# Memory recalls in products of 64 features, two halves of TensorE's rows at a time, and three sums of x moved to GpSimd

## The chip, the cores and the metric

One core of one Trainium2 chip runs the whole program. The metric is the device time of one execution in microseconds (us), the median of several runs. TensorE multiplies, VectorE, ScalarE and GpSimd work on tiles, SyncE issues the transfers.

## What is computed

`x` has 2048 rows (tokens) and 576 columns (features). The output mixes two branches by a gate per token:

```python
g = sigmoid((x * gate_w).sum(-1, keepdims=True))
out = g * A(x) + (1 - g) * B(x)          # B: (gelu(x @ w_gate) * (x @ w_up)) @ w_down, 4608 wide
```

`A` is attention with 32 heads of 18 features, in 4 segments of 512 tokens, with a memory that is carried from segment to segment:

```python
phi = lambda t: where(t > 0, t + 1.0, exp(t))
M, z = zeros, zeros                       # per head: 18 x 18 and 18
for s in range(4):
    a_dot = softmax(qs @ ks.T * scale + mask) @ vs          # within the segment
    a_mem = (phi(qs) @ M) / (phi(qs) @ z + 1e-6)            # the recall
    outs.append(sigmoid(beta) * a_mem + (1 - sigmoid(beta)) * a_dot)
    M = M + phi(ks).T @ vs
    z = z + phi(ks).sum(0)
A = concat(outs) @ wo
```

The recall `phi(qs) @ M` and its denominator `phi(qs) @ z` are what the change touches.

## The kernel before

The program begins with the projections. For each segment `s` from 1 on there are four "rows" steps (`q` = 0 to 3, 128 tokens each), in which the values are projected (`vrows`, `put_rows`), the key features of the segment before are turned (`key_rows`) and added to the memory (`memorize`), and the recall of the segment before is made (`recall(p, q)` with `p = s - 1`); then nine products `project(s, j)` give the columns of q and k, which `put_columns` splits into f16 words and turns into `phi`. The recalls of segment 3 come last: two together in step `j = 6`, one in `j = 7`, one after `j = 8`. Segment 0 has no memory to recall, so there are 3 x 4 = 12 recalls. After the projections the feed-forward branch and the attention run together in `step(v)` to the end; the first `step` begins with `first_product`, whose result in the PSUM bank V VectorE copies out (L1339) before more is added to V.

All four compute engines follow the order in which the program text issues (`manual_schedule`). `later` is a list of closures: work on a product's result is put there and issued at the next `finish_later()`.

For the recall, the 576 features lie in five tiles of 128 partitions (`SPANS`). `phi[s, j]` holds tile `j` as fp32, 128 features x 512 tokens; the fifth has the last 64 features of q in its upper half and the first 64 of k, for which `bd` is zero, in its lower. `bd[:, j]` holds, as fp32, the memory of the heads that tile `j` touches, block by block: for each of up to 8 heads (`HEADS`) 18 columns of `M` and one of `z` (`MC` = 19), zero outside the head's own features. One recall is five products with 128 tokens of `phi` as weights and 152 columns of `bd` (76 for the last tile) streaming. Tiles 0 to 2 add up in one PSUM bank, 3 and 4 in another; head 21 lies in both, and `put_recall` adds its two parts, then forms denominators, reciprocals and scaled results, which go to DRAM (`oms`).

`form_sums(p, i, half, by)` makes sums of x for later products: a subtraction of 1024 columns on the engine `by` (L482), a cast by ScalarE (L484), the low words by VectorE (L486). `half` says which of these: 0 the subtraction and the cast, 1 the low words, 2 the cast alone, -1 the subtraction alone. `beside_rows` and `behind_rows` call it in the rows steps. PSUM has eight banks: `st` and `dn` two each, G, U, V and `pv` one each.

The functions that the diff touches, with the lines of the profile:

Of the kernel before, what the change touches and what calls it, by code (L numbers as in the profile page):

```python
# [8 lines left out]
F32 = mybir.dt.float32  # L9
# [4 lines left out]
OP = mybir.AluOpType  # L14
# [4 lines left out]
P = 128  # L19
D = 576  # L20
F = 4608
H = 32
DH = 18
L = 512
NH = D // 2
KT = 5
# [11 lines left out]
GN = 20  # L38
MC = DH + 1
SPANS = [(128 * j, min(128, D - 128 * j)) for j in range(KT)]  # L40
HS = 21
HEADS = [(a // DH, (a + w - 1) // DH + 1) for a, w in SPANS]


# [1 line left out]
def kernel(ctx: ExitStack, tc: tile.TileContext, xs, wqk, wv, wo, wgu, wd, beta, out):  # L46
    nc = tc.nc
    pe, act, dve, pool, sp = nc.tensor, nc.scalar, nc.vector, nc.gpsimd, nc.sync
# [425 lines left out]
    def form_sums(p, i, half, by=dve):  # L474

        r, sc = sums_x[p], xsc[:, 2 * p : 2 * p + 1]
        t = kept["xt"][p] if half >= 0 else None
        k, o, a, b = ((0, (1, 1), (1, 2), (1, 1)), (2, (1, 2), (2, 2), (1, 2)), (1, (2, 2), (2, 2), (1, 1)))[i]
        if t is not None:
            hi, lo = (flat(t[:, 4 * k + j : 4 * k + j + 2]) for j in (0, 2))  # L480
        if half <= 0:
            by.tensor_tensor(r[o], r[a], r[b], OP.subtract)  # L482
        if half == 0 or half == 2:
            act.activation(hi, r[o], AF.Copy, scale=sc)  # L484
        if half == 1:
            dve.scalar_tensor_tensor(lo, r[o], sc, hi, OP.mult, OP.subtract)  # L486
# [12 lines left out]
    qks, vps, oms, oas = [], [], [], []  # L499
# [8 lines left out]
    gh = cst.tile([P, 2, H], F32, name="gh")  # L508
# [17 lines left out]
    with tc.tile_pool(name="prj", bufs=2, side="right", reuse_waits="tile") as pp:  # L526
# [10 lines left out]
        W, phi, vst, kr, mem = {}, {}, {}, {}, {}  # L537
# [139 lines left out]
        def recall(s, q, banks=(("st", 2), ("st", 2))):  # L677

            na, nb = (bank(*i) for i in banks)

            for j, (h0, h1) in enumerate(HEADS):
                o, lo = (na, 0) if j < 3 else (nb, HS)
                pe.matmul(o[:, (h0 - lo) * MC : (h1 - lo) * MC], phi[s, j][:, q * P : (q + 1) * P],
                          bd[:, j, : (h1 - h0) * MC], start=j in (0, 3), stop=j in (2, 4), skip_group_check=True)
            later.append(lambda: put_recall(s, q, na, nb))

        def put_recall(s, q, na, nb):
            hf, c = divmod(s, 2)
            t = 4 * c + q
            dn = pp.tile([P, H], F32, name="den", bufs=2)  # L690
            rd = pp.tile([P, H], F32, name="rden", bufs=2)
            mo = pp.tile([P, D], F32, name="mo", bufs=2)
            both = na[:, HS * MC : (HS + 1) * MC]
            dve.tensor_copy(mo[:, :MC], nb[:, :MC])
            dve.tensor_tensor(both, both, mo[:, :MC], OP.add)
            parts = []
            for o, h0, h1 in ((na, 0, HS + 1), (nb, HS + 1, H)):
                o = o[:, (MC if h0 else 0) :][:, : (h1 - h0) * MC]
                parts.append((o.rearrange("p (h d) -> p h d", d=MC), slice(h0, h1), h1 - h0))
            for o, hs, n in parts:  # L700
                dve.tensor_scalar(dn[:, hs].unsqueeze(2), o[:, :, DH:], 1e-6, None, OP.add)
            dve.reciprocal(rd, dn)
            dve.tensor_tensor(rd, rd, gh[:, 0], OP.mult)
            for o, hs, n in parts:
                dve.tensor_tensor(mo[:, hs.start * DH : hs.stop * DH].rearrange("p (h d) -> p h d", d=DH), o[:, :, :DH],
                                  rd[:, hs].unsqueeze(2).to_broadcast([P, n, DH]), OP.mult)
            sp.dma_start(oms[hf][t * P : (t + 1) * P, :], mo)

        def key_rows(s, q):
            ka, kb = bank("G") if s else bank("st", 2), bank("V")  # L710
# [66 lines left out]
        with tc.manual_schedule(engines=ORDERED):  # L777
# [91 lines left out]
            def beside_rows(s, q):  # L869
                if 0 < s < 3 and q == 0:  # L870
                    add_squares(s, range(1, KT))
                if s == 1 and q == 1:
                    add_squares(0, range(1, KT))
                if s == 1 and q == 0:
                    load_sums(0)
                if s == 1 and q == 2:
                    rescale(0)
                    rescale_words(0)
                if s == 2:
                    if q > 1:  # L880
                        form_sums(0, q - 2, 1)
                    if q:
                        form_sums(0, q - 1, 0)
                if s == 3 and q == 0:
                    rescale(2)
                    for i in range(2):
                        squares(0, 1, i, lambda o, r: square_sum(o, r, True))
            def behind_rows(s, q):
                if s == 3:
                    if q == 1:  # L890
                        scales(0)
                        scales_out(0)
                        scale_g(0)
                        scale_g(1)
                    if q < 3:
                        form_sums(1, q, -1, pool if q == 0 else dve)
                    if q == 3:
                        rescale_words(2)
                        high_g(0, 0)
                        low_g(0, 0)  # L900
# [91 lines left out]
            for s in range(4):  # L992
                p = s - 1
                if s:
                    for q in range(4):
                        pv = vrows(s, q, 0)
                        if q == 0:
                            key_scale(p)
                        if done:
                            put_columns(*done)  # L1000
                            done = None
                        finish_later()
                        put_rows(s, q, 0, *pv)
                        if s == 3 and q == 0:
                            norm_x(3, bank("V"))
                        if q:
                            key_rows(p, q - 1)
                        beside_rows(s, q)
                        finish_later()
                        if held:  # L1010
                            held.pop()()
                        behind_rows(s, q)
                        pv = vrows(s, q, 1)
                        put_rows(s, q, 1, *pv)
                        if p >= 1:
                            recall(p, q)
                        if q:
                            memorize(p, q - 1)
                    finish_later()
                    key_rows(p, 3)  # L1020
                for j in range(9):
                    if j == 1 and s:
                        make_gate(s)
                    if s and j == 0:
                        memory_scale(p)
                    if s or j > 1:
                        pr = project(s, j)
                    elif j == 0:
                        prs = project_first()
                        pr = prs[0]  # L1030
                    else:
                        pr = prs[1]
                    if s and j == 0:
                        finish_later()
                        memorize(p, 3)
                    if s == 0 and j in (2, 3, 5, 6):
                        make_qk(j + 2 + (j == 3))
                    if done and (s, j) != (0, 1):
                        for d in done if isinstance(done, list) else [done]:
                            put_columns(*d)  # L1040
                    done = [done, pr] if (s, j) == (0, 1) else pr
                    if s and j == 1:
                        keep_memory(p)
                    if s == 3 and j == 1:

                        first.close()
                        mp2 = stay.enter_context(tc.tile_pool(name="ffn2", bufs=2, reuse_waits="tile"))
                        xt.append(mp2.tile([P, 12, L], F16, name="xt1", bufs=1))
                        home.update(r=mp2)
                    beside_products(s, j)  # L1050
                    finish_later()
                    if (s, j) == (1, 3):
                        make_gate(0)
                    if s == 0 and j >= 6:
                        q = j - 5
                        pv = vrows(0, q, 1)
                        put_rows(0, q, 1, *pv)
                    if s == 3 and j == 6:
                        recall(3, 0, (("dn", 2), ("dn", 2)))
                        recall(3, 1, (("V",), ("pv",)))  # L1060
                    if s == 3 and j == 7:
                        recall(3, 2, (("dn", 2), ("dn", 2)))
# [766 lines left out]
```

## Time and profile before

| | |
|---|---|
| runs | 1555.67 us median of 3 (1555.64 to 1556.55) |
| the profiled execution | span 1553.8 us from its first to its last instruction; the profile gives no other time of it |
| TensorE (PE) | busy 1548.4 us, 12195 matmul entries |
| weight loads (PEld) | busy 955.7 us, beside the matmuls |
| VectorE (DVE) | busy 1229.3 us |
| ScalarE (ACT) | busy 1183.7 us |
| GpSimd (POOL) | busy 1305.8 us |

Times in the profile are us from the start of the span. A matmul's entry lasts until its modelled end, so entries of successive matmuls overlap; the distance from one start to the next is what a matmul costs. In a group, `out<-in` are the program's tiles, `128*128` the array's rows and columns in use, then the streaming operand. Brackets in a timeline give idle time of the engine before a row and what ended it.

### The profile page before, as it was taken

How to read it: one execution, taken by the hardware profiler on the slowest of the kernel's cores; microseconds unless marked ns; L12 is line 12 of the kernel's file. 1: busy time of each engine (PE TensorE's matmuls, PEld its weight loads, DVE VectorE, ACT ScalarE, POOL GpSimd, SP SyncE). 2: the span in 40 equal slices, each digit the busy share in tenths (PEclk: the TensorE clock that was granted, in tenths of full speed). 3: DMA queues.
4: the chain of work that ended last, by engine and by line, in shares of the span. 5: the costliest groups of instructions: out<-in, count | busy, mean ns of one | idle time of the engine just before them, and what ended most of it. 6: DMA issues, size and time to landing. Idle time of an engine off the chain costs nothing.

```text
span 1553.8 us, 33925 instructions
## 1 busy us (share of the span) xinstructions
PE 1548.4 (100%) x12195; PEld 955.7 (62%) x12196; DVE 1229.3 (79%) x3198; ACT 1183.7 (76%) x2037; POOL 1305.8 (84%) x1313
## 2 busy tenths in 40 slices
PE   9999999999999999999999999999999999999999
PEld 5665655666666566666666665666666666666577
DVE  6788976778878887878788887878787878887665
ACT  7567544888888888888888888888888888876421
POOL 3544778899898999989899989898999989899597
PEclk9999999999999999999999999999999999999999
DMA  7533341667768687778777878878687878774654
GB/s 254 195 127 125 132 150 34 122 126 140 133 131 141 130 144 130 144 126 137 132 136 126 140 139 136 135 140 151 127 138 133 144 128 141 130 136 99 120 118 138
DMA packets 472601, 210.14 MB, mean 135 GB/s; under 512 B 427632, under 2 KB 437360, under 8 KB 471920
## 3 DMA queue, kind: packets, MB, share of 16 engines
q1 hardware_dynamic: 472432, 207.97, 67.6%
q8 instruction: 96, 1.57, 0.4%
q14 instruction: 73, 0.60, 0.1%
HBM read 92.03 MB, written 27.26 MB: 77 GB/s over the span
## 4 chain that ended last, share of the span: by engine, by line
PE 94%; POOL 3%; ACT 2%; DVE 1%; issue 1%; POOLq 0%
PE dn L1228 27%; PE U L1268 22%; PE V L1268 12%; PE pv L1183 4%; PE G L385 3%; PE st L447 3%; PE dn L454 2%; PE U L1275 2%; PE dn L385 1%; PE U L447 1%; PE V L1280 1%; PE G L1280 1%; PE st L1137 1%; PE G L447 1%; PE st L1669 1%; PE V L1275 1%
## 5 line engine op out<-in xcount | busy, mean ns | idle before, releaser
L1228 PE MATMUL dn<-paird,hh 128*128 128x288 f16 x3396 | 476.5, 286 | 0.2
L1164 POOL TENSOR_TENSOR pf<-pf,ph 128x512 f16<-128x512 f32 (+1 forms) x256 | 359.2, 1403 | 94.6 <-ACT ph L1163 83.6
L1228 PEld LDWEIGHTS <-hh 128*128 128x128 f16 x3456 | 332.2, 98 | 139.1 <-issue 18.1
L1268 PEld LDWEIGHTS <-pairg 128*128 128x128 f16 x2616 | 244.0, 98 | 254.8 <-issue 18.3
L1236 DVE SCALAR_TENSOR_TENSOR acc<-dn,ev,acc 128x288 f32<-128x288 f32 x534 | 274.4, 515 | 51.4 <-PE dn L1228 42.9
L1153 ACT ACTIVATE pf<-pf,mb,esc 128x512 f32<-128x512 f32 (+3 forms) x512 | 293.0, 642 | 5.2
L1268 PE MATMUL U<-xt,pairg 128*128 128x512 f16 x864 | 209.9, 379 | 0.2 <-DVE gl L1459 0.2
L1268 PE MATMUL U<-x,pairg 128*128 128x512 f16 x840 | 204.1, 379 | 0.0
L426 POOL TENSOR_TENSOR pairg<-raw,pairg 128x640 f16<-128x640 f32 (+2 forms) x144 | 176.2, 1239 | 3.0 <-ACT pairg L418 1.5
L1163 ACT ACTIVATE ph<-pf 128x512 f16<-128x512 f32 (+1 forms) x256 | 172.4, 720 | 0.0
L1255 POOL TENSOR_TENSOR hh<-gl,hh 128x512 f16<-128x512 f32 x144 | 164.4, 1163 | 7.5 <-ACT hh L1254 7.5
L1140 DVE CUSTOM_DVE_ANT_0 pf<-st,mask 128x512 f32<-128x512 f32 (+1 forms) x256 | 157.2, 614 | 0.0
L418 ACT ACTIVATE pairg<-raw 128x640 f16<-128x640 f32 (+2 forms) x144 | 89.3, 647 | 56.6 <-POOL raw L410 36.2
L1258 ACT ACTIVATE gl<-gl,sc 128x512 f32<-128x512 f32 x144 | 97.2, 716 | 40.7 <-DVE gl L1505 30.1
L303 POOL TENSOR_SCALAR raw<-raw,sc 128x640 f32<-128x640 f32 x72 | 118.7, 1663 | 0.0
L1459 DVE COPY gl<-U 128x512 f32<-128x512 f32 x72 | 49.8, 692 | 85.4 <-PE U L1268 74.9
L1150 ACT ACTIVATE mb<-mx,esc 128x4 f32<-128x4 f32 x128 | 37.5, 293 | 103.4 <-DVE mx L1140 103.4
L1140 DVE CUSTOM_DVE_ANT_0 pf<-dn,mask 128x256 f32<-128x256 f32 (+1 forms) x192 | 67.2, 375 | 55.3 <-PE dn L1137 55.3
L1268 PE MATMUL V<-xt,pairg 128*128 128x512 f16 x432 | 105.7, 381 | 0.0
L1268 PE MATMUL V<-x,pairg 128*128 128x512 f16 x432 | 104.8, 378 | 0.0
L1254 ACT ACTIVATE hh<-gl 128x512 f16<-128x512 f32 x144 | 82.6, 616 | 16.0 <-DVE gl L1250 15.8
L1183 PEld LDWEIGHTS <-pt 128*128 128x128 f16 x2560 | 83.4, 96 | 12.3
(354 smaller groups left out, 2971.1 us busy)
## 6 DMA issues: line engine op xcount, KB each, us to landing
raw<-in_wgu_dram SPq DMA_DIRECT2D x36, 640.0 KB
rawd<-in_wd_dram SPq DMA_DIRECT2D x36, 288.0 KB
qk<-stage SPq DMA_DIRECT2D x36, 256.0 KB
qt<-qk SPq DMA_DIRECT2D x128, 72.0 KB
kt<-qk SPq DMA_DIRECT2D x128, 72.0 KB
vp<-vstage SPq DMA_DIRECT2D x16, 296.0 KB
vt<-vp SPq DMA_DIRECT2D x16, 296.0 KB
qt<-qk SPq DMA_DIRECT2D x128, 36.0 KB
```

The costliest lines, as they stand in the source:

```text
L303: pool.tensor_scalar(r, r, scl[f // 2][0][:, 0:1], None, OP.mult)
L426: pool.tensor_tensor(spot(f, *p, 1), raw_g[f][:, p[0] : p[1]], spot(f, *p, 0), OP.subtract)
L1140: dve.tensor_tensor_reduce(prob[a][:, COL[qi] : COL[qi] + (qi + 1) * P], out[qi], mask[:, L - (qi + 1) * P :], 1.0, -3e38, OP.add, OP.max, ...
L1153: act.activation(r, r, AF.Exp, bias=b[:, qi : qi + 1], scale=esc[:, 0, c : c + 1])
L1163: act.activation(h[:, cols], p[:, cols], AF.Copy)
L1164: pool.tensor_tensor(p.bitcast(F16)[:, cols], p[:, cols], h[:, cols], OP.subtract)
L1183: pe.matmul(ov, pr[:, 10 * i + COL[qi] // P + kb], v[:, 4 * e + kb, c0 : c0 + VC], start=kb == 0 and i == 0, stop=kb == qi and i == 1)
L1228: pe.matmul(o[:, :NH], hh[:, a, q * P : (q + 1) * P], w[:, b, n * NH : (n + 1) * NH], start=i == 0, stop=i == 5)
L1236: dve.scalar_tensor_tensor(av, o[:, :NH], ev, av, OP.mult, OP.add)
L1255: pool.tensor_tensor(hh[:, 1], t, hh[:, 0], OP.subtract)
L1258: act.activation(t, o, AF.Gelu_apprx_tanh, scale=scl[f // 2][0][:, 2 + c : 3 + c])
L1268: pe.matmul(o, w[:, i, (a + k) * P : (a + k + 1) * P], x[:, b + k], start=start and k == 0 and i == 0 and b == h, stop=k == 1 and i == 1, ...
```

## The change

Each product of 128 features becomes two of 64: features 0 to 63 of a tile (upper half of the array's rows) add up in bank `na`, 4 heads or 76 columns each, and features 64 to 127 in bank `nb`, 5 heads or 95 columns each; the last tile has an upper half alone. So a recall has nine products of 64 rows in place of five of 128. Every tile now has its own place in both banks, and the heads that two halves share (first and last of the five in `nb`) are added in `put_recall`: a copy of 152 columns (by ScalarE for segments 1 and 2, by VectorE for segment 3) and two adds of 76. Denominators and results are taken through views of 35 places, since the banks repeat heads in groups of 7.

Three subtractions of `form_sums` go from VectorE to GpSimd: those of sums 1 and 2 of the first pair of segments (rows steps 2 and 3 of segment 2) and of sum 1 of the second pair (rows step 1 of segment 3, now ahead of the scales). In segment 2 the cast is issued behind the second `put_rows` instead of with the subtraction.

```diff
-            for j, (h0, h1) in enumerate(HEADS):
-                o, lo = (na, 0) if j < 3 else (nb, HS)
-                pe.matmul(o[:, (h0 - lo) * MC : (h1 - lo) * MC], phi[s, j][:, q * P : (q + 1) * P],
-                          bd[:, j, : (h1 - h0) * MC], start=j in (0, 3), stop=j in (2, 4), skip_group_check=True)
+            tok = slice(q * P, (q + 1) * P)
+            for j in range(KT):
+                for h, o, c, n in ((slice(0, 64), na, 0, 4 * MC), (slice(64, P), nb, 3 * MC, 5 * MC))[: 2 if j < 4 else 1]:
+                    pe.matmul(o[:, j * n : (j + 1) * n], phi[s, j][h, tok], bd[h, j, c : c + n],
+                              start=j == 0, stop=j == (4 if c == 0 else 3), skip_group_check=True)
...
-            both = na[:, HS * MC : (HS + 1) * MC]
-            dve.tensor_copy(mo[:, :MC], nb[:, :MC])
-            dve.tensor_tensor(both, both, mo[:, :MC], OP.add)
...
+            ga = na[:, : 20 * MC].rearrange("p (g e d) -> p g e d", g=5, e=4)
+            gb = nb[:, : 20 * MC].rearrange("p (g e d) -> p g e d", g=4, e=5)
+            cut = mo[:, : 8 * MC].rearrange("p (g e d) -> p g e d", g=4, e=2)
+            (act.copy if s < 3 else dve.tensor_copy)(cut, gb[:, :, 0::4])
+            for e in range(2):
+                o = ga[:, e : e + 4, 3 * (1 - e)]
+                dve.tensor_tensor(o, o, cut[:, :, e], OP.add)
+            by = lambda t: t.rearrange("p (g e) -> p g e", e=7)
+            parts = (ga, slice(0, 5), slice(0, 4)), (gb[:, :, 1:4], slice(0, 4), slice(4, 7))
...
                     if q:
-                        form_sums(0, q - 1, 0)
+                        form_sums(0, q - 1, -1, pool if q > 1 else dve)
...
                 if s == 3:
+                    if q < 2:
+                        form_sums(1, q, -1, pool)
                     if q == 1:
                         scales(0)
                         scales_out(0)
...
-                    if q < 3:
-                        form_sums(1, q, -1, pool if q == 0 else dve)
+                    if q == 2:
+                        form_sums(1, q, -1)
...
                         put_rows(s, q, 1, *pv)
+                        if s == 2 and q:
+                            form_sums(0, q - 1, 2)
                         if p >= 1:
                             recall(p, q)
```

## Rows read from the trace of the kernel before

**Rows 1.** The page's chain that ended last, shares of the span by engine.

```profile
PE 94%; POOL 3%; ACT 2%; DVE 1%; issue 1%; POOLq 0%
```

**Rows 2.** Busy times by stretch: us, busy per engine (x instructions), clock, DMA.

```profile
178.00:212.40 34.40, 34.38 (x188) 18.81 (x186) 32.99 (x65) 22.15 (x37) 21.98 (x19) 1.00 0.41 135
```

**Rows 3.** TensorE's timeline, recalls at 102 and 172 us: start us, us, what.

```profile
102.21 1.37 PE L683 MATMUL st<-bd,phi 128*128 128x152 f32 x10
103.42 0.29 PE L454 MATMUL U<-wv,x 128*128 128x288 f16 x1
...
172.08 1.37 PE L683 MATMUL st<-bd,phi 128*128 128x152 f32 x10
```

**Rows 4.** Weight loads at the end of the recall at 197 us.

```profile
197.97 0.19 PEld L683 LDWEIGHTS dn<-bd,phi 128*128 128x128 f32 x1
198.08 0.30 PEld L683 LDWEIGHTS V<-bd,phi 128*128 128x128 f32 x2
```

**Rows 5.** TensorE's timeline, fp32 products with 128 and with 64 rows.

```profile
12.92 0.65 PE L674 MATMUL pv<-acc,raw 128*128 128x288 f32 x2
...
14.08 0.40 PE L674 MATMUL V<-acc,raw 64*128 64x288 f32 x1
14.09 0.40 PE L674 MATMUL pv<-acc,raw 64*128 64x288 f32 x1
14.33 0.40 PE L674 MATMUL V<-acc,raw 64*128 64x288 f32 x1
...
14.66 0.76 PE L674 MATMUL G<-acc,raw 128*128 128x290 f32 x2
```

**Rows 6.** Weight loads of the products with 64 rows.

```profile
13.49 0.30 PEld L674 LDWEIGHTS dn<-acc,raw 64*128 64x128 f32 x4 [0.39 <-issue]
13.84 0.19 PEld L674 LDWEIGHTS V<-acc,raw 64*128 64x128 f32 x1
```

**Rows 7.** TensorE's timeline, end of the projections.

```profile
196.93 1.37 PE L683 MATMUL dn<-bd,phi 128*128 128x152 f32 x10
...
199.40 3.19 PE L447 MATMUL U<-x,wp 128*128 128x512 f16 x14
202.60 1.45 PE L683 MATMUL dn<-bd,phi 128*128 128x152 f32 x10
...
210.71 1.46 PE L1268 MATMUL V<-x,pairg 128*128 128x512 f16 x6
```

**Rows 8.** VectorE's timeline, last rows step.

```profile
171.11 0.68 DVE L724 SCALAR_TENSOR_TENSOR krow<-G,kmc,krow 128x448 f16<-128x448 f32 x1 [0.19 <-ACT krow L720]
...
173.79 0.17 DVE L694 COPY mo<-st 128x19 f32<-128x19 f32 x1
```

**Rows 9.** VectorE's timeline, end of the projections.

```profile
200.57 0.16 DVE L694 COPY mo<-dn 128x19 f32<-128x19 f32 x1
200.76 0.18 DVE L695 TENSOR_TENSOR dn<-dn,mo 128x19 f32<-128x19 f32 x1
200.98 0.26 DVE L701 TENSOR_SCALAR den<-dn 128x22 f32<-128x22 f32 x2
...
203.05 0.18 DVE L701 TENSOR_SCALAR den<-V 128x22 f32<-128x22 f32 x1
...
209.94 0.68 DVE L1339 COPY gl<-V 128x512 f32<-128x512 f32 x1
...
213.93 0.69 DVE L1459 COPY gl<-U 128x512 f32<-128x512 f32 x1 [1.97 <-PE dn L99]
```

**Rows 10.** ScalarE's groups, 98 to 125 us: busy us, mean ns, idle.

```profile
L720 ACT ACTIVATE krow<-V,kmc 128x128 f16<-128x128 f32 x4 | 1.4, 359 | 0.0
```

**Rows 11.** Line 482, the sums: duration ns min/median/max, first and last start.

```profile
L482 DVE TENSOR_TENSOR acc<-acc x5: 1217/1218/1364, 105.7 to 166.2; 128x1024 f32<-128x1024 f32 x5
L482 POOL TENSOR_TENSOR acc<-acc x1: 2352/2352/2352, 155.5 to 155.5; 128x1024 f32<-128x1024 f32 x1
```

**Rows 12.** Waits between 95 and 260 us: total us, times, longest us.

```profile
POOL sc L275 <- DVE v L268: 11.4, 2, 8.2
```

More of the change, by code (lines that the diff above doesn't have):

```diff
@@ L40 @@
 SPANS = [(128 * j, min(128, D - 128 * j)) for j in range(KT)]
-HS = 21
 HEADS = [(a // DH, (a + w - 1) // DH + 1) for a, w in SPANS]
@@ L689, in put_recall @@
             t = 4 * c + q
-            dn = pp.tile([P, H], F32, name="den", bufs=2)
-            rd = pp.tile([P, H], F32, name="rden", bufs=2)
-            mo = pp.tile([P, D], F32, name="mo", bufs=2)
-            both = na[:, HS * MC : (HS + 1) * MC]
-            dve.tensor_copy(mo[:, :MC], nb[:, :MC])
-            dve.tensor_tensor(both, both, mo[:, :MC], OP.add)
[L696 to L707, printed above, removed]
+            dn = pp.tile([P, 35], F32, name="den", bufs=2)
@@ new lines, in put_recall @@
+            rd = pp.tile([P, 35], F32, name="rden", bufs=2)
+            mo = pp.tile([P, 35 * DH], F32, name="mo", bufs=2)
+            ga = na[:, : 20 * MC].rearrange("p (g e d) -> p g e d", g=5, e=4)
[5 more added lines that the diff above has]
+                dve.tensor_tensor(o, o, cut[:, :, e], OP.add)
@@ new lines, in put_recall @@
+            by = lambda t: t.rearrange("p (g e) -> p g e", e=7)
+            parts = (ga, slice(0, 5), slice(0, 4)), (gb[:, :, 1:4], slice(0, 4), slice(4, 7))
+            for o, g, e in parts:
+                dve.tensor_scalar(by(dn)[:, g, e], o[:, :, :, DH], 1e-6, None, OP.add)
+            dve.reciprocal(rd[:, :H], dn[:, :H])
+            dve.tensor_tensor(rd[:, :H], rd[:, :H], gh[:, 0], OP.mult)
+            for o, g, e in parts:
+                n = o.shape[1], o.shape[2]
+                dve.tensor_tensor(mo.rearrange("p (g e d) -> p g e d", e=7, d=DH)[:, g, e], o[:, :, :, :DH],
+                                  by(rd)[:, g, e].unsqueeze(3).to_broadcast([P, *n, DH]), OP.mult)
@@ L709, in key_rows @@
+            sp.dma_start(oms[hf][t * P : (t + 1) * P, :], mo[:, :D])
         def key_rows(s, q):
```

## Prediction

> **What bounds the kernel now.** I read the page's chain that ended last first: 94% of it is TensorE [rows 1]. So an edit counts if it changes what TensorE does, or makes it wait. The twelve recalls lie between 102 and 208 us. The table of busy times of the last of them, 178 to 212.4 us, has the granted clock at 1.00 (2.4 GHz), TensorE at 34.38 of 34.40 us, and VectorE at 32.99 [rows 2]: two engines are full there. That second one is easily missed.
>
> Next the timeline of TensorE. One recall runs from 102.21 to the next product's start at 103.42: 1.21 us [rows 3]. It has ten entries for five products, so an fp32 product is two passes. The price of a pass comes from the fp32 products of 288 columns at 14 us: 14.33 - 14.08 = 0.243 us [rows 5], or 0.84 ns a column. Eight passes of 152 columns are then 8 x 0.128, two of 76 columns 2 x 0.064, together 1.15; the recall takes 0.06 more. The weight loads say why: at the end of the recall at 197 us they start at 197.97, 198.08 and (198.08 + 0.30 - 0.19) 198.19, so 0.111 apart, although a pass of 76 columns streams in 0.064 [rows 4]. So an fp32 weight load sets a floor of 0.111 us under every pass. 152 columns lie above that floor, 76 below.
>
> **What the change does, part by part.** *The products.* Every pass gets narrower: 76 columns in the upper half, 95 in the lower (0.064 and 0.080 us), while there are ten passes above and eight below instead of ten in all. Do the halves run side by side in fp32? Yes: at 14.08 and 14.09 two products of 64 rows start in two banks, and their second passes at 14.33 [rows 5]. And their loads too: four loads of 64 rows begin within 13.49 to (13.49 + 0.30 - 0.19) 13.60, that is two pairs 0.11 apart [rows 6]. So loads in the two halves don't add up, but a load of 64 rows takes as long as one of 128. The upper half's ten passes are then ten loads.
>
> Going to halves and back costs as well. The pass before the halves starts at 12.92 + 0.24 and ends streaming at 13.40; the first half starts at 13.49: 0.095 us. Back: 14.33 + 0.24 = 14.57, and the next starts at 14.66: 0.095 again [rows 5]. The first load after the switch is not hidden: 13.84 - 13.49 = 0.35 = 0.11 + 0.24 [rows 6].
>
> Sum for a recall alone: 0.095 + 0.11 + 9 x 0.111 + 0.064 + 0.095 = 1.36, and 0.01 for the first f16 load behind it: 1.37 against 1.21, **+0.165 us**. Bounds: +0.12 to +0.20 as the rounding of the floor allows (0.106 to 0.115), and -0.27 if passes streamed without it (0.095 + 0.11 + 760 x 0.84 ns + 0.095 = 0.94). I take the floor, since rows 4 and 6 show it in either mode. Two recalls in a row (196.93 to 199.40, 2.47 us [rows 7]) pay the switch once: 0.095 + 0.11 + 19 x 0.111 + 0.064 + 0.105 = 2.48, +0.01.
>
> The Trainium skill ("TensorE: Matmul & The Clock Gate", section LDWEIGHTS (loading the stationary operand)) says the load goes by columns, not by rows, and gives columns / 1.2 ns, an estimate of 107 ns for 128 columns; the 0.11 us of rows 4 and 6 agrees, and by it the sum of a recall would be 1.33. The Trainium skill (same page, Measured speedup vs the span model) prices a pack at the duration of a matmul and 4 ns per tile; by that rule the recall would be faster, which is rival A.
>
> *The evacuation.* Before: a copy of 19 columns, an add, then the denominators: 200.57 to 200.98, 0.41 us [rows 9]. After: a copy of 152 columns and two adds of 76. VectorE's copies go from 0.17 us at 19 columns to 0.68 at 512 [rows 8, 9], 1.03 ns a column: the copy is 0.17 + 133 x 1.03 ns = 0.31, each add 0.18 + 57 x 1.03 ns = 0.24. Between dependent operations lie 0.04 us (200.98 - 200.76 - 0.18); two independent ones overlap (two denominators take 0.26 where one takes 0.18 [rows 9]), so the second add ends an estimated 0.16 behind the first. That is 0.31 + 0.04 + 0.24 + 0.16 + 0.04 = 0.79, **+0.38 us** on VectorE for each of the four recalls of the last segment. Bounds: +0.1 (fixed costs alone, one more instruction overlapped) to +0.7 (no overlap, a slower read of the strided columns). For the other eight the copy is ScalarE's, about 0.38 us (its 128 columns take 0.359 [rows 10]); VectorE keeps 0.44 against 0.41 but waits for the copy. That is hidden: the bank is next written a whole row later, some 6 us. Denominators, reciprocal and scaling keep their element counts; the stores on SyncE's queue stay as many and wait with VectorE.
>
> *The sums.* Three subtractions leave VectorE (1.218 us each) for GpSimd (2.352 us) [rows 11]. All stand where VectorE later waits for other engines anyway (0.19 us at 171.11 for the last time [rows 8]), so what it gains ends there: 0. On GpSimd's queue the third one comes to stand ahead of the scales of the first weights, before which GpSimd now idles 11.4 - 8.2 = 3.2 us [rows 12], enough for 2.35; the other two meet a nearly empty queue. Without that room each would cost 1.13, the difference of the engines. The ScalarE cast that goes with a sum is moved behind the second row cast, with the same duration: 0.
>
> **Where it meets.** VectorE's last wait before the end of this part is at 171.11 us, for ScalarE's half of the key words, which wait for TensorE; from there to 211.96 it runs without a gap, and idles 1.97 us only at 213.93 [rows 8, 9]. So from 171 on its lateness only grows: 7 x 0.165 = 1.16 from the recalls before it; the evacuation of 173.79 must then wait for the cut (the recall of 172.08 ends at 173.45 [rows 3], + 0.165, + 0.04, + ScalarE's 0.38, + 0.04, so its adds start at 174.08), +0.29; then 4 x 0.38 = 1.52. Together 2.97. Behind these adds on VectorE's queue stand the low words of the keys, for which the memory's products wait: in a row they come up to 0.3 late, TensorE itself 0.165; at most 0.14 us of new wait, and no more at the end, as VectorE sets that. Who waits for VectorE? First the recall at 202.60, which needs banks that the evacuation of 200.57 frees; it waits already (its first pass lags: 1.45 us for ten passes against 1.37) [rows 7]. Then the product into V at 210.71, which may only add to V when the copy of 209.94 has read it, at 210.62 [rows 7, 9]: no slack but the hand-over. TensorE by itself would be there 8 x 0.165 + 0.01 + 0.165 = 1.5 late, or 2.0 with the wait at 202.60. VectorE sets it: +2.97. From 213.93 on VectorE waits for TensorE again [rows 9], and all that follows shifts by the same: **+3.0 us**. Span 1553.8 + 2.97 = 1556.8. The median of the runs, 1555.67, lies 1.9 us above the span, which I take as what lies around it: 1555.67 + 2.97 = 1558.6, +0.19%. What a measurement of this kernel can tell from no change is about 0.2%, 3.1 us, so the forecast lies just inside that bound.
>
> **Rivals.** *A, halves that stream:* if the loads of a half hid under the other half's passes, a recall would be 0.94 us, -0.27. For it: the pairs of rows 5. Against: the pairs of loads 0.11 apart, and the floor of rows 4. Even then VectorE decides: 7 x -0.27 = -1.9, no wait for the cut, + 4 x 0.38 + 0.02 = -0.4: 1555.3.
> *B, loads that don't overlap the same half's pass:* each pass 0.11 + 0.064 = 0.174, a recall 0.095 + 1.74 + 0.105 = 1.94, +0.73; the pair +1.2; with ten single ones +8.5: **1564, slower**. It decides from about 0.13 us a pass on. The Trainium skill (same page, The mechanism) lets a load overlap only a pass in another row group. Rows 5 and 6 speak against it: V's first load starts at 13.84 and its pass at 14.08, just the 0.24 that the pass of the same rows before it streams.
> *C, the evacuation is cheap or hidden:* VectorE catches up (an operation slowed by GpSimd between 179 and 200 us runs faster), and TensorE's own +1.5 is left: 1557.2.
> *D, the evacuation costs the upper bound:* 4 x 0.7 + 1.46 = +4.3: **1560.0, slower**.
>
> **How the numbers follow.** Forecast 0.45 (its own range 1557.6 to 1559.6, so just over half within 0.2%), A 0.10, C 0.17, D 0.17, B 0.06; 0.05 is left for a gain that no row shows. Faster by over 0.2%: 0.05. Within: 0.10 + 0.17 + 0.24 = 0.51. Slower: 0.21 + 0.17 + 0.06 = 0.44. The range from 1555.2 to 1561.2 takes in A, C, D and leaves out B and the unseen gain.
>
> **What would show it.** Right: weight loads of one half 0.11 us apart in the recall, a recall of 1.35 to 1.40 us in the rows, gaps of 0.095 ahead of and behind it; a wait of about 0.9 us ahead of the third product behind the last recall (V), for VectorE's copy; VectorE's copy of 152 columns at 0.3 us. Wrong: a recall under 1.1 us (A) or over 1.8 (B), no wait at V (C), evacuations over 0.6 us longer (D), or TensorE waiting for VectorE in the rows, between 102 and 178 us.

## The result, and the profile after

The changed kernel takes 1562.43 us (median of 5 runs, 1562.27 to 1564.03) against 1555.67: 6.8 us more, ratio 1.0040 with a 95% interval of 1.0029 to 1.0051. So it is slower by more than the 0.2% that can be told from no change, and lies above the forecast of 1558.6 and above the range's end of 1561.2. The profiled span grew from 1553.8 to 1560.8 us.

The page's chain that ended last, shares of the span by engine, answers to [rows 1]:

```profile
PE 90%; DVE 3%; POOL 3%; ACT 2%; issue 1%; DMA 0%; DVEq 0%; POOLq 0%
```

TensorE lost four hundredths of the chain, and two of them are VectorE's now: TensorE waits for it where it did not before. Two timelines, of TensorE and of its weight loads, show the recall itself, which answers to [rows 3] and [rows 6] (start us, us, what, and in brackets the idle time before):

```profile
102.41 0.29 PE L456 MATMUL dn<-wv,x 128*128 128x290 f16 x1
102.63 1.33 PE L683 MATMUL st<-bd,phi 64*128 64x76 f32 x18
103.89 1.28 PE L453 MATMUL U<-wv,x 128*128 128x288 f16 x9
```

```profile
102.62 1.19 PEld L683 LDWEIGHTS st<-bd,phi 64*128 64x128 f32 x18 [0.24 <-POOL phi L628]
```

The f16 product ahead streams its 290 columns until 102.41 + 0.12 = 102.53. The first half starts 0.10 later, and the next product at 103.89: the recall takes 1.36 us where it took 1.21. That is what was forecast. The large waits stand elsewhere, in TensorE's timeline further on:

```profile
124.30 0.68 PE L740 MATMUL U<-vstage,krow 128*128 128x152 f16 x7 [1.54 <-DVE krow L727]
...
164.31 1.41 PE L683 MATMUL st<-bd,phi 64*128 64x76 f32 x18 [1.00 <-DVE mo L708]
...
208.04 1.33 PE L683 MATMUL dn<-bd,phi 64*128 64x76 f32 x18 [0.42 <-DVE mo L708]
...
217.69 1.46 PE L1275 MATMUL V<-x,pairg 128*128 128x512 f16 x6 [0.97 <-DVE gl L1346]
```

The last two were spoken of in the prediction. The first two, 2.5 us together, were not, or not at this size: a memory product that waits for the low words of the keys (at most 0.14 us was forecast), and a recall that waits for its bank. VectorE was late for both, and its own timeline says why. Each pair below is VectorE's product of the reciprocals with the gate, and GpSimd's sum in the same moment:

```profile
111.46 1.75 DVE L705 TENSOR_TENSOR rden<-rden,gh 128x32 f32<-128x32 f32 x1
...
118.11 1.71 DVE L705 TENSOR_TENSOR rden<-rden,gh 128x32 f32<-128x32 f32 x1
119.85 0.82 DVE L708 TENSOR_TENSOR mo<-st,rden 128x360 f32<-128x360 f32 x2
120.59 2.69 DVE L485 SCALAR_TENSOR_TENSOR xt<-acc,xsc,xt 128x1024 f16<-128x1024 f32 x1
...
161.22 2.38 DVE L705 TENSOR_TENSOR rden<-rden,gh 128x32 f32<-128x32 f32 x1
```

```profile
110.80 2.36 POOL L481 TENSOR_TENSOR acc<-acc 128x1024 f32<-128x1024 f32 x1
...
117.42 2.35 POOL L481 TENSOR_TENSOR acc<-acc 128x1024 f32<-128x1024 f32 x1
119.85 2.35 POOL L490 TENSOR_TENSOR acc<-acc 128x1024 f32<-128x1024 f32 x1
...
161.21 2.35 POOL L481 TENSOR_TENSOR acc<-acc 128x1024 f32<-128x1024 f32 x1
```

The product has 32 columns and lasts 0.19 us at 209.75 (below). Here it ends at 113.21, 119.82 and 163.60, and GpSimd's sums at 113.16, 119.77 and 163.56: each time 0.04 to 0.05 us behind the sum, whenever it began. It doesn't run slowly, it stands until the sum has ended. The scaling of 119.85 (L708), longer by far, runs beside the next GpSimd instruction undisturbed; it reads its first operand from PSUM, while the product and the low words (L485, 2.69 us) read two tensors from SBUF. The loss of the first stand-still is taken up before it reaches TensorE; the two others and the 2.69 us become the waits at 124.30 and 164.31.

### The profile page after: what moved, and what is told of

Its sections match the earlier page's. It is cut to its first block, busy times and chain, and to the rows that moved or that the text cites. A ratio compares the mean times of both kernels' runs of the same rounds, so it can differ in the third digit from the quotient of the medians.

```text
span 1560.8 us, 34147 instructions
## 1 busy us (share of the span) xinstructions
PE 1551.3 (99%) x12291; PEld 954.2 (61%) x12292; DVE 1235.8 (79%) x3199; ACT 1185.9 (76%) x2045; POOL 1312.3 (84%) x1316
## 4 chain that ended last, share of the span: by engine, by line
PE 90%; DVE 3%; POOL 3%; ACT 2%; issue 1%; DMA 0%; DVEq 0%; POOLq 0%
PE dn L1235 27%; PE U L1275 22%; PE V L1275 12%; PE pv L1190 4%; PE G L384 3%; PE U L1282 2%; PE st L446 2%; PE dn L453 2%; PE dn L384 1%; PE G L1287 1%; PE V L1287 1%; PE st L1144 1%; PE st L1676 1%; PE V L1282 1%; PE G L1282 1%
```

## The experiments

The eight kernels were run in two sets of four, beside 27 and 31 runs of the kernel before (1555.84 and 1555.93 us).

| kernel | median us (runs) | ratio to before, 95% interval |
|---|---|---|
| e1_sums_back: halves, sums as before | 1559.34 (11) | 1.0023 (1.0014 to 1.0032) |
| e2_sums_only: recalls as before, sums moved | 1559.03 (11) | 1.0017 (1.0008 to 1.0026) |
| e3_psum_operand: the change, reciprocals in PSUM | 1559.38 (11) | 1.0022 (1.0013 to 1.0031) |
| e4_wide_upper: the change, 128 columns above | 1562.86 (1) | none, one run |
| e5_no_join: e1 without the join | 1557.65 (11) | 1.0010 (1.0001 to 1.0019) |
| e6_cut_on_act: e1, cut by ScalarE throughout | 1560.34 (9) | 1.0027 (1.0017 to 1.0037) |
| e7_sums_psum: e2, reciprocals in PSUM | 1555.89 (11) | 0.9998 (0.9989 to 1.0007) |
| e8_psum_alone: before, reciprocals in PSUM | 1556.07 (11) | 0.9999 (0.9990 to 1.0008) |

### The two parts by themselves

e1 takes the edits of the sums out of the changed kernel; e2 makes them alone in the kernel before:

```diff
-                        form_sums(0, q - 1, 0)
+                        form_sums(0, q - 1, -1, pool if q > 1 else dve)
...
+                    if q < 2:
+                        form_sums(1, q, -1, pool)
...
-                    if q < 3:
-                        form_sums(1, q, -1, pool if q == 0 else dve)
+                    if q == 2:
+                        form_sums(1, q, -1)
...
+                        if s == 2 and q:
+                            form_sums(0, q - 1, 2)
```

> The recall in halves as changed, the three sums on VectorE as before. Theory (in the changed kernel VectorE's product of the reciprocals with the gate, two operands in SBUF, stands still while GpSimd works on a sum: 1.75 us at 111.46 and 2.38 us at 161.22 instead of 0.19): without the sums on GpSimd these stand-stills go, and with them the waits of TensorE behind them (0.23 + 0.33 + 1.71 + 1.15 = 3.4 us between 109 and 165 us): 1558.6 to 1559.6 us, the last wait at V stays at about 1 us. Rival (the new evacuations alone make VectorE late, whoever forms the sums): the waits between 109 and 165 us stay, 1561.5 us or more, since VectorE then also has the sums of 1.22 us.

> The recall and its evacuation as before, only the three sums moved to GpSimd and the cast behind the second row cast. Theory (stand-still of VectorE beside GpSimd): line 705's counterpart, the product of reciprocals and gate, takes 1.5 to 2.4 us in the three rows steps where GpSimd forms a sum, TensorE waits for the low words of the keys and once for the recall's banks: slower by 2 to 4 us, 1557.7 to 1559.7. Rival (moving the sums costs nothing or relieves VectorE, as forecast): 1555.4 to 1556.

Measured: 1559.34 and 1559.03 us. Either part costs some 3 us alone, 3.5 and 3.2; together they cost 6.5 (against 1555.93) to 6.8 (against 1555.67), so within the spread of the runs they add. In e1 the waits for the key words at 124 us and for the bank at 164 us are gone; this is what is left in its timeline of TensorE:

```profile
205.46 1.33 PE L683 MATMUL dn<-bd,phi 64*128 64x76 f32 x18 [0.42 <-DVE mo L708]
...
214.75 1.46 PE L1271 MATMUL V<-x,pairg 128*128 128x512 f16 x6 [0.62 <-DVE gl L1342]
```

In e2, whose recalls are those of before, the same two waits stand as in the changed kernel, and the same product is blown up:

```profile
PE U L737 <- DVE krow L724: 1.7, 1, 1.7
PE st L683 <- DVE mo L705: 1.4, 1, 1.4
```

```profile
L703 DVE TENSOR_TENSOR rden<-rden,gh x12: 192/193/2307, 104.5 to 213.1; 128x32 f32<-128x32 f32 x12
```

(First the waits: total us, times, longest; then the product on line 703: shortest, median and longest ns.) 1.7 + 1.4 = 3.1 us of waits against 3.2 us of loss: the sums' price is these two waits, and the halves have no part in it. Three of the eleven runs of e2 took only 1557.0 to 1557.6 us, which is why its ratio is below that of the medians; the profile is of one of the other eight, and what those three save is not seen.

### The operand

Is it the two operands in SBUF, or only that GpSimd is busy? e3 writes the reciprocals to free columns of the recall's bank, so that the product reads one operand there:

```diff
-            dve.reciprocal(rd[:, :H], dn[:, :H])
-            dve.tensor_tensor(rd[:, :H], rd[:, :H], gh[:, 0], OP.mult)
+            ri = na[:, 20 * MC : 20 * MC + H]
+            dve.reciprocal(ri, dn[:, :H])
+            dve.tensor_tensor(rd[:, :H], ri, gh[:, 0], OP.mult)
```

> The changed kernel, but the reciprocals are written to free columns of the recall's PSUM bank and read from there, so the product with the gate has only one operand in SBUF. Theory (two operands in SBUF make VectorE stand still): this product takes 0.2 us in every step although GpSimd forms the sums at the same places, the waits at 116, 124 and 164 us go or shrink below 0.4 us each: 1558.5 to 1559.8. Rival 1 (any VectorE instruction is slowed while GpSimd runs): the product stays at 1.7 to 2.4 us, 1562.4. Rival 2 (the evacuations' adds and ScalarE's copy make VectorE late): 1562.0 to 1562.6 with the product at 0.2 us.

Measured: 1559.38 us, 3.05 less than with the operand in SBUF, and the same as e1. VectorE's and GpSimd's timelines at the first of the three places, and the product's durations by bank:

```profile
111.21 0.19 DVE L706 TENSOR_TENSOR rden<-st,gh 128x32 f32<-128x32 f32 x1
111.44 0.82 DVE L709 TENSOR_TENSOR mo<-st,rden 128x360 f32<-128x360 f32 x2
112.17 1.82 DVE L485 SCALAR_TENSOR_TENSOR xt<-acc,xsc,xt 128x1024 f16<-128x1024 f32 x1
```

```profile
110.55 2.37 POOL L481 TENSOR_TENSOR acc<-acc 128x1024 f32<-128x1024 f32 x1
```

```profile
L706 DVE TENSOR_TENSOR rden<-st,gh x9: 174/192/192, 105.2 to 214.1; 128x32 f32<-128x32 f32 x9
```

The sum runs from 110.55 to 112.92 just as before, and the product in its midst takes 0.19 us. The low words at 112.17, still with two operands in SBUF, are held too: they take 1.82 where the shortest took 1.27, and end 1.07 us behind the sum. The Trainium skill ("SBUF — State Buffer", section Who interferes with whom) has this as a rule: a VectorE instruction with two inputs in SBUF contends with a GpSimd instruction that reads SBUF, one with at most one such input, outside VectorE's two-port modes, doesn't. The traces here agree on both halves of it, 1.7 to 2.4 us against 0.19.

e7 makes the same edit in e2, and e8 in the kernel before:

```diff
-            dve.reciprocal(rd, dn)
-            dve.tensor_tensor(rd, rd, gh[:, 0], OP.mult)
+            ri = na[:, (HS + 1) * MC : (HS + 1) * MC + H]
+            dve.reciprocal(ri, dn)
+            dve.tensor_tensor(rd, ri, gh[:, 0], OP.mult)
```

> The kernel before with the three sums on GpSimd, and the reciprocals written to PSUM, so that their product with the gate reads one operand from SBUF and one from PSUM. Theory: the sums cost only because this product stands still beside them; with the operand in PSUM the product lasts 0.19 us, TensorE's waits for the key words at 123 us and for the bank at 163 us go, and the time is that of the kernel before, 1555.4 to 1556.4 us. Rival: the sums also cost by their own 1.1 us longer duration on GpSimd, or by slowing other VectorE instructions: 1557.5 us or more.

> The kernel before with the reciprocals in PSUM and nothing else changed. Theory: before, the longest of the twelve products lasted 0.67 us and none made TensorE wait, so the operand's place is worth nothing there: 1555.3 to 1556.2 us. Rival: the place of the operand by itself is what made the third kernel faster (by 3.0 us), sums or not: 1553 to 1554.5 us.

Measured: 1555.89 and 1556.07 us, both the time of the kernel before. So the three sums on GpSimd, the moved cast included, cost 3.2 us with the operand in SBUF and nothing with it in PSUM, and the edit by itself gains nothing. e7 is the only version here that keeps a part of the change without a loss; it does not beat the kernel before.

### The halves

Rival A had it that narrow passes gain. e4 makes the upper eight passes wider, 128 columns in place of 76; the columns added multiply by zeros:

```diff
-                    pe.matmul(o[:, j * n : (j + 1) * n], phi[s, j][h, tok], bd[h, j, c : c + n],
+                    w = 128 if c == 0 and j < 4 else n
+                    pe.matmul(o[:, j * n : j * n + w], phi[s, j][h, tok], bd[h, j, c : c + w],
```

> The changed kernel, but eight of the ten passes of the upper half stream 128 columns instead of 76 (the added columns of the memory are zero in these rows and add nothing). Theory (a weight load of 0.111 us is the floor of every pass): 128 columns stream in 0.107 us, so the recall stays at its length of 1.37 us, passes 0.111 apart. Rival (streaming sets the length of a recall in halves): eight passes 0.043 us longer, the recall 1.7 us, the kernel +3 to +4 us.

Measured once: 1562.86 us, and a recall of the same length, in TensorE's timeline:

```profile
102.49 1.34 PE L684 MATMUL st<-bd,phi 64*128 64x128 f32 x18
103.76 0.91 PE L453 MATMUL U<-wv,x 128*128 128x288 f16 x6
```

From 102.49 to 103.76 it is 1.27 us, with 76 columns 102.63 to 103.89, 1.26. Most of the upper passes stream two thirds more and the recall is no longer: the columns don't space them, and the weight loads fit. In either kernel the eighteen loads of a recall take 1.19 us; with 0.19 for one of them as the trace has it [rows 4], the ten of the upper half start (1.19 - 0.19) / 9 = 0.111 us apart.

What remains of e1's 3.5 us is then the halves themselves or the longer evacuation. e5 leaves the join out of e1: the copy and the two adds for the eight heads that lie in both halves.

```diff
-            (act.copy if s < 3 else dve.tensor_copy)(cut, gb[:, :, 0::4])
-            for e in range(2):
-                o = ga[:, e : e + 4, 3 * (1 - e)]
-                dve.tensor_tensor(o, o, cut[:, :, e], OP.add)
```

> The sums stand on VectorE as before; the recalls go in halves, but the eight heads that lie in both halves are not joined (the copy and the two adds are left out, so these heads hold the sum of the lower half's bank alone). Theory: of the 3.5 us that halves and their evacuation cost together, TensorE's own share is ten times about 0.16 us (eight recalls in the rows, two single ones at the end) plus some 0.2 us of variation at the start; the rest is the longer evacuation, which makes TensorE wait for the low words of the keys (0.24, 0.32, 0.32 us) and at the product into V (0.79 us). Without the join these waits go: 1557.0 to 1557.9 us. Rival: the halves themselves delay the banks or the queue behind them, and the evacuation is innocent: 1559.0 or more, the waits unchanged.

Measured: 1557.65 us, within the theory's numbers. TensorE's timeline has no wait for VectorE at the end of the projections any more, V included:

```profile
208.10 1.33 PE L683 MATMUL st<-bd,phi 64*128 64x76 f32 x18
209.37 1.47 PE L1266 MATMUL V<-xt,pairg 128*128 128x512 f16 x6
210.68 1.46 PE L1266 MATMUL G<-x,pairg 128*128 128x512 f16 x6
212.09 1.46 PE L1266 MATMUL V<-x,pairg 128*128 128x512 f16 x6
```

So the halves cost TensorE 1557.65 - 1555.93 = 1.7 us, and the join as much again, 1559.34 - 1557.65 = 1.7. Each difference is about as large as the half-width of these intervals (0.0009, or 1.4 us). That they are real rests on the runs, which do not overlap (the kernel before beside e5 up to 1557.28, e5 1557.35 to 1558.00, e1 from 1558.95), and on the traces, where the waits come and go with the edit.

e6 gives the copy of the last segment to ScalarE as well, in e1:

```diff
-            (act.copy if s < 3 else dve.tensor_copy)(cut, gb[:, :, 0::4])
+            act.copy(cut, gb[:, :, 0::4])
```

> The sums stand on VectorE as before; the copy of the 152 columns is ScalarE's in all segments, the last one too. Theory: VectorE's longer evacuation in the last segment sets the wait at the product into V; with 0.31 us less on VectorE for each of four recalls that wait falls from 0.79 to under 0.3 us, and the time from 1559.3 to 1558.5 to 1559.0 us. Rival: VectorE then stands waiting for ScalarE's copy just as long, so the wait at V stays: 1559.3 us, same.

Measured: 1560.34 us (1559.22 to 1561.41), by the median slower than either theory said. The profiled execution took 1559.31 us, which is the rival's time. In it, VectorE's, ScalarE's and TensorE's timelines:

```profile
203.16 0.53 DVE L699 TENSOR_TENSOR dn<-dn,mo 128x76 f32<-128x76 f32 x2 [1.27 <-ACT mo L696]
...
206.58 1.38 DVE L705 TENSOR_TENSOR rden<-rden,gh 128x32 f32<-128x32 f32 x1
```

```profile
201.32 0.74 ACT L93 ACTIVATE junk<-raw 128x640 bf16<-128x640 f32 x1 [2.18 <-DVE stat L89]
201.96 0.18 ACT L93 ACTIVATION_READ_ACCUMULATOR junk<-raw 128x1 f32 x1
202.18 0.68 ACT L93 ACTIVATE junk<-rawd 128x576 bf16<-128x576 f32 x1
202.77 0.19 ACT L93 ACTIVATION_READ_ACCUMULATOR junk<-rawd 128x1 f32 x1
202.86 0.27 ACT L696 COPY mo<-dn 128x152 f32<-128x152 f32 x1
```

```profile
205.30 1.41 PE L683 MATMUL dn<-bd,phi 64*128 64x76 f32 x18 [1.28 <-DVE mo L708]
```

The copy stands in ScalarE's queue behind statistics of the next weights, which wait 2.18 us for VectorE. So VectorE waits 1.27 us for ScalarE, and TensorE 1.28 us for the bank, where it was 0.42. The wait at V did vanish, as the theory had it, but a larger one took its place. In this execution the product also stood still once more (1.38 us), beside a GpSimd instruction that works on weights. What makes the slowest of these runs 2 us slower than the fastest is not seen in the one profile and stays open.

## Why the prediction was wrong, step by step

**The step that failed is "The sums": "what it gains ends there: 0".** It moved three sums from one queue to another and priced them by their durations and the room on GpSimd's queue. Those were right: the sums last 2.35 us, and e7 shows that they cost nothing as such. The room that was counted on ahead of the scales, 3.2 us [rows 12], is used in e7 as forecast: 9.2 - 8.3 = 0.9 us of it are left. In the changed kernel 13.2 - 10.4 = 2.8 are left, since VectorE, whose work the scales wait for, is late itself (total us, times, longest; first e7, then the changed kernel):

```profile
POOL sc L275 <- DVE v L268: 9.2, 2, 8.3
```

```profile
POOL sc L274 <- DVE v L267: 13.2, 2, 10.4
```

What was missing is what VectorE does meanwhile: its product of 0.19 us lasts up to 2.38 us beside the sum. The measured term is 1562.43 - 1559.34 = 3.1 us. Added to the forecast, it alone takes the time beyond the range (1558.6 + 3.1 = 1561.7). The side of the 0.2% would have been missed without it: e1, at 1559.34, already lies 0.23% above the kernel before, by the evacuation below. No rival held the term. The prediction did name its sign, TensorE waiting for VectorE between 102 and 178 us, as one of those that would show it wrong.

The trace of before held a hint. The same product on its line there, and the low words (shortest, median and longest ns):

```profile
L703 DVE TENSOR_TENSOR rden<-rden,gh x12: 191/193/672, 104.7 to 209.8; 128x32 f32<-128x32 f32 x12
...
L486 DVE SCALAR_TENSOR_TENSOR xt<-acc,xsc,xt x6: 1275/1556/1940, 111.2 to 192.1; 128x1024 f16<-128x1024 f32 x6
```

One shape with durations that differ by half or by a factor of three points to an instruction that something else holds up.

**The recall in halves** was right: 1.37 us forecast, 1.36 measured; the load floor of 0.111 us, the gap of 0.10 ahead, both halves' loads side by side. TensorE by itself was to come 1.5 us late; e5 gives 1.7. Rivals A and B fall with it.

**The evacuation** was right in mechanism and too small. VectorE's timeline in the last segment, to be held against [rows 9]:

```profile
205.43 0.30 DVE L696 COPY mo<-dn 128x152 f32<-128x152 f32 x1
205.83 0.53 DVE L699 TENSOR_TENSOR dn<-dn,mo 128x76 f32<-128x76 f32 x2
206.39 0.26 DVE L703 TENSOR_SCALAR den<-dn 128x20 f32<-128x20 f32 x2
...
209.75 0.19 DVE L705 TENSOR_TENSOR rden<-rden,gh 128x32 f32<-128x32 f32 x1
...
215.88 0.53 DVE L699 TENSOR_TENSOR st<-st,mo 128x76 f32<-128x76 f32 x2 [0.46 <-DVE mo L696]
```

From the copy to the denominators it is 206.39 - 205.43 = 0.96 us, where 0.79 was forecast and 0.41 stood before: +0.55 instead of +0.38. The copy was right (0.30 for 0.31); the two adds take 0.53 for an estimated 0.40, and 0.10 us lie between copy and adds, not 0.04. With 0.55 the prediction's own sum is 1.16 + 0.29 + 4 x 0.55 = 3.65, or 1559.3, and e1, which is the change without the sums, measured 1559.34. That agreement is luck, since two further terms were off. The memory products were to wait at most 0.14 us in a row, and none of it was to reach the end. TensorE's timeline of the same nine products of a row, first in e1, then in e5:

```profile
115.77 1.13 PE L740 MATMUL U<-vstage,krow 128*128 128x152 f16 x9
```

```profile
115.15 0.81 PE L735 MATMUL U<-vstage,krow 128*128 128x152 f16 x9
```

With the join they take 0.32 us longer: a wait of a third of a microsecond for the low words, which stand behind the join on VectorE's queue. In e1 the weight loads of these products wait three times so (total us, times, longest), in e5 never:

```profile
PEld L740 <- DVE krow L727: 1.0, 3, 0.3
```

So the evacuations of the rows steps were not hidden either. The other term is the 0.29 us that VectorE was to wait for ScalarE's copy in the last rows step. Its timeline there in e1 shows no idle time:

```profile
175.93 0.21 DVE L655 TENSOR_SCALAR gate<-dn,al 128x1 f32<-128x1 f32 x1
176.06 0.52 DVE L699 TENSOR_TENSOR st<-st,mo 128x76 f32<-128x76 f32 x2
```

These adds stand where the copy at 173.79 stood before [rows 8], 2.27 us later, where 1.16 + 0.29 = 1.45 was forecast: VectorE comes so late that it finds the copy ready. Rival C (the evacuation is hidden) falls with this and with the wait at V. Rival D had +0.7 for each evacuation, and its 1560.0 comes nearest to e1; to the changed kernel's 1562.43 rival B's 1564 is nearer, by a recall of 1.94 us that did not occur.

**Where it meets** was right in kind: the waits at the bank (208.04, 0.42 us) and at V (217.69, 0.97 us; about 0.9 was forecast) are there, VectorE sets them, and e5 shows that the join does. In the changed kernel VectorE idles 0.46 us between its last copy and the adds at 215.88, which adds to the latter; in e1 it is 0.10, and the wait at V 0.62. In e3, whose product does not stand still, it is 0.46 again, so the stand-still is not what holds these adds; what does was not tried.

The whole loss by its causes, from the medians: TensorE's own passes 1.7 (e5), the join 1.7 (e1 - e5), the stand-still 3.1 (changed kernel - e1). Their sum, 6.5, is 1562.43 - 1555.93 by the way they are formed; that these are the causes is shown by the waits that go with e5 and by e3 and e7.

## What to carry to other kernels

That GpSimd has room does not make it free to move an elementwise sum there: first list what VectorE runs in that stretch, and how many of its operands lie in SBUF. Here a short VectorE instruction with two of them, in a chain that frees a bank, paid all that was left of the GpSimd instruction; one operand in PSUM took the price away. And the fp32 products here, whose passes stream for less time than lies between two weight loads (0.064 against 0.111 us), gained nothing from a split into halves: compare the stream of one pass with the spacing of the loads first.

## What was not expected of the hardware

- A VectorE instruction of 32 columns with two operands in SBUF lasted 0.19 us alone and up to 2.38 us beside a GpSimd sum, ending 0.04 to 0.05 us behind it in all three cases; with one operand in PSUM it lasted 0.19 us beside the same sum.
- Two adds of 76 strided columns in PSUM, independent of each other, took 0.53 us as a pair, and started 0.10 us behind the copy that they need, where a copy and an add of 19 columns had 0.03 between them (200.57 + 0.16 to 200.76 [rows 9]).
